# Two transformer layers in fp32: the last quarter of the tokens is transposed on VectorE instead of TensorE ahead of each feed-forward

## The chip, the core and the metric

The kernel runs on one core of a Trainium2 chip. A core has five engines with an instruction queue each: TensorE (PE in the profile; its weight loads are listed apart as PEld), VectorE (DVE), ScalarE (ACT), GpSimd (POOL) and SyncE (SP, which here only issues DMAs). Each engine works through its own queue in order and waits on semaphores for the others. The time is the device time of one execution in microseconds (us), the median of several runs.

## What is computed

Two layers, each attention with shared keys and values (16 query heads, one key/value head) and a SwiGLU feed-forward, both behind a layer norm and added to the residual. S = 2048 tokens, width D = 448, head width 28, feed-forward width F = 1792, all fp32.

```python
def _A_ref(x, wq, wk, wv, wo):                  # attention, one k and v for 16 heads
    q = (x @ wq).reshape(B, S, H, Dh).transpose(0, 2, 1, 3)
    k, v = x @ wk, x @ wv
    p = softmax(einsum("bhqd,bkd->bhqk", q, k) * Dh ** -0.5)
    return einsum("bhqk,bkd->bhqd", p, v).transpose(0, 2, 1, 3).reshape(B, S, H * Dh) @ wo

def _B_ref(x, w_gate, w_up, w_down):            # SwiGLU
    return (silu(x @ w_gate) * (x @ w_up)) @ w_down

x = A_x
for _ in range(2):                              # the same weights in both layers
    x = x + _A_ref(layernorm(x), wq, wk, wv, wo)
    x = x + _B_ref(layernorm(x), w_gate, w_up, w_down)
```

## The kernel before

**Numbers in two parts.** The products run on operands of a shortened fp32 type (fp32r in the rows), so each operand is split into a high part (`xh`, a cast) and a low part (`xl`, what the cast lost), and a product is three passes: high x high, high x low, low x high. To split a 512-token block is called halving it here (`halved`, lines L292 to L302: a cast and a subtraction for each of the quarters k = 0, 1, 2 of the width; for k = 3, only 64 rows wide, two casts and one subtraction).

**Tokens.** The residual `xres` stays in SBUF, tokens on the partitions, as 16 tiles of 128 x 448. Four tiles make a chunk c = 0 to 3 of 512 tokens. For the feed-forward a chunk has to be normed and transposed (width on the partitions). There are two ways. One goes over TensorE: `flip` transposes 128 x 128 blocks with an identity into a PSUM bank (L248), and ACT and VectorE halve from the bank (L254 to L264). The other goes over VectorE and DRAM: `turn_tile` transposes within 32 x 32 squares (L268), `send` writes the result to DRAM so that the squares land in place (L274, four DMAs), and `fetch` reads it back (`rows3`, L130 and L132). Tokens then stand in another order, and `natural` and `in_order` put them right with strided views where a bank is read.

**Norm.** `norm_steps` gives nine steps: statistics of four tiles (L217, L218 on VectorE), the scale on GpSimd (L222, L223), and the application to four tiles (L230, VectorE). Where the chunk goes over TensorE, GpSimd also copies 64 columns a second time behind each (L232).

**Feed-forward.** F is cut into 14 tiles fc of 128, two to a group gi (7 groups). The loops run over group, chunk and tile of the group: `unit(gi, c, n)` computes gate and up for one tile of F and one chunk into a pair of PSUM banks (L332, in two halves of 64 rows side by side; between them two one-element copies by ACT, L339, keep the order). Then ACT takes Silu (L1021), VectorE multiplies (L1022), ACT casts the high part (L1023), VectorE subtracts for the low part `h` (L1026). The down product of a unit (also L332, operands `wdh`, `wdl` and `h`) isn't issued at once: it is kept in `pend` and stands in the middle and at the end of the next unit. After the second tile of a group four banks hold a sum of 128 x 448 each, which is added to the residual: tiles 0 and 1 by VectorE (L892), tiles 2 and 3 by a copy of ACT (L895) and an addition of GpSimd (L896). These additions stand on their engines between the Silu work of the next unit.

**Banks.** PSUM has eight banks. Gate and up take turns over LOW = (0, 1, 2, 3), the down sums hold HIGH = (4, 5, 6, 7). `bank()` hands out the next bank of a list; TensorE waits there until its former user has let go.

**Order.** The schedule is written by hand: within an engine the instructions stand in the order of the code. `soon` holds steps that are run some units later, `mid` steps that stand in the middle of a certain unit, `plan` steps of the hand-over between the layers.

**Chunk 3.** Chunks 0 to 2 have gone over VectorE and DRAM during attention and are ready early. Chunk 3's residual is only complete when attention ends. In `rest`, at the start of the feed-forward, its statistics are taken; chunk 2 is halved by GpSimd (`parts(2)`); chunk 3 is applied two units later, by `soon`; and in the middle of unit (0, 2, 1), before and after the first half of the down product, TensorE transposes it (`turned`), two blocks of eight 128 x 128 blocks. The first unit that reads it is (0, 3, 0). Chunk 3 is therefore the only one whose tokens stand in the natural order (`sq` is false for it).

**Projections of layer 1.** During the last units of layer 0's feed-forward, and after it in `finish`, queries, keys and values of layer 1 are computed, 16 projections of 128 rows (`q`, products L312). Each holds one bank, which ACT copies out (and VectorE too, L546, where it holds a part of v). In `finish` of layer 1 the banks come from a list that begins with bank 0.

Of the kernel before, what the change touches and what calls it, by code (L numbers as in the profile page):

```python
# [55 lines left out]
def forward(  # L56
# [286 lines left out]
    class Attention:  # L343
# [79 lines left out]
        def parts(self, i):  # L423
            q = qts[i % 3]
            split(q[:, 0, :], q[:, 1, :], qraw)
# [86 lines left out]
        def turned(self, c):  # L512
            if c in self.norms:
                flip(self.norms.pop(c), self.X[c])

        def q(self, c, m):
            cs = slice(512 * c, 512 * c + 512)
            sq = c in self.squares
            held, po = bank((3, 4, 5) if self.seen > len(self.order) - 4 else wide[-1], True)
            ms = slice(P * m, P * m + P)  # L520
            wh, wl = self.w
# [31 lines left out]
        def finish(self):  # L553

            wide.append((0, 1, 2, 3, 4, 5, 6, 7) if self.layer else ALL)
            if self.layer:
# [280 lines left out]
    class FeedForward:  # L837
# [132 lines left out]

        def turned(self, c, ks=range(4)):
            if c not in self.X:
                self.X[c] = xtile(self.xbp, self.xd[c])
            flip(self.norms[c], self.X[c], ks)

        def flush(self):
# [5 lines left out]
        def unit(self, gi, c, n):  # L982
# [36 lines left out]
            sg = pers.tile([P, 512], F32, name="sg")  # L1019
            sq = c < NC - 1  # L1020
            nc.scalar.activation(in_order(sg, sq), natural(pg[0], sq), AF.Silu)  # L1021
            nc.vector.tensor_tensor(in_order(sg, sq), natural(pg[1], sq), in_order(sg, sq), ALU.mult)  # L1022
            nc.scalar.copy(hh, sg)  # L1023
# [34 lines left out]
        def rest(self, xb):  # L1058
# [4 lines left out]
            for c in range(2):  # L1063
                dma(self.xd[c][64:128, :], self.X[c][0][0:64, 3, :])
                self.X[c] = (*self.X[c][:2], self.xd[c])
            fs3, self.norms[3] = norm_steps(3)
            for f in fs3[:5]:
                f()
            self.parts(2, nc.gpsimd.tensor_copy, nc.gpsimd.tensor_tensor)
            self.soon.append([1, lambda: [f() for f in fs3[5:]]])  # L1070
            self.mid[0, 2, 1] = [lambda ks=ks: self.turned(3, ks) for ks in ((0, 1), (2, 3))]
            for gi, fs in enumerate(groups):
# [4 lines left out]
                for c in range(NC):  # L1077
                    for n in range(len(fs)):
                        if gi or c:
                            self.unit(gi, c, n)  # L1080
                if gi == len(groups) - 2 and self.nxt:
                    self.nxt.w = load_wqkv(xb.enter_context(tc.tile_pool(name="wqkv1", bufs=1, reuse_waits="tile")), None)[1]
# [87 lines left out]
```

## Times and profile before

| | us |
|---|---|
| median of 3 runs (lowest to highest) | 1957.98 (1957.88 to 1958.28) |
| profiled execution | 1958.55 |
| its span | 1956.8 |
| TensorE busy | 1942.8 (99%) |
| TensorE weight loads busy | 1328.7 (68%) |
| VectorE busy | 969.6 (50%) |
| ScalarE busy | 1262.7 (65%) |
| GpSimd busy | 553.9 (28%) |
| attention and projections of layer 0, 0 to 564: TensorE busy | 559.0 |
| feed-forward of layer 0, 564 to 974: TensorE busy | 409.2 of 410 |
| attention of layer 1, 974 to 1533: TensorE busy | 556.5 of 559 |
| feed-forward of layer 1 and end, 1533 to 1957: TensorE busy | 418.1 of 424 |

The limits of the four stretches are round numbers near the places where one kind of work ends and the next begins. The feed-forward of layer 1 repeats that of layer 0 about 968.8 us later, so one of them is read in detail and the other checked. Rows of the time order give start, duration, engine, line, operation, output and inputs; "x4" are four like instructions that follow each other, and "[0.36 <-DVE sg L1022]" is the time that the engine stood idle before the row and what released it. Ends of rows overlap the next start by some hundredths, since an engine starts the next instruction before the last one has drained.

### The profile page before, as it was taken

The numbers are of one execution on the slowest core, as the hardware profiler recorded it, in microseconds if no ns is written. First come the engines' busy times: TensorE is split into PE (matmuls) and PEld (weight loads), VectorE is DVE, ScalarE is ACT, GpSimd is POOL, SyncE is SP. The second block draws the span as 40 slices with busy tenths as digits, with TensorE's granted clock in tenths as the row PEclk, the third lists the DMA queues.
The fourth block names the chain that finished last, engine by engine and source line by source line (L and its number), as shares of the span: only waits on it lengthen the run. The fifth ranks groups of instructions, "written<-read, shape, count | busy, mean of one in ns | idle before, by whom it ended". The sixth has DMA issues, their size and how long they took to land. (4 is left out here: it accounts for less than half of the span.)

```text
span 1956.8 us, 43898 instructions
## 1 busy us (share of the span) xinstructions
PE 1942.8 (99%) x18425; PEld 1328.7 (68%) x18425; DVE 969.6 (50%) x1639; ACT 1262.7 (65%) x1877; POOL 553.9 (28%) x592
## 2 busy tenths in 40 slices
PE   9999999999999999999999999999999999999998
PEld 7544545445468999999974445454454789988887
DVE  6666575665643222322655555657656432232323
ACT  4899898998953333333349998989989333333332
POOL 4213123122214333433341221122231342333420
PEclk9999999999999999999999999999999999999999
DMA  5111011121130011100251110110221201011102
GB/s 167 55 35 30 21 39 41 27 55 39 25 87 25 17 32 32 33 22 22 70 156 36 34 34 20 42 38 24 57 50 32 72 18 31 17 32 32 32 1 77
DMA packets 100642, 83.60 MB, mean 43 GB/s; under 512 B 25080, under 2 KB 81656, under 8 KB 100440
## 3 DMA queue, kind: packets, MB, share of 16 engines
q1 hardware_dynamic: 98744, 79.32, 14.7%
q8 instruction: 145, 2.38, 0.5%
q10 hardware_dynamic: 1696, 1.43, 0.2%
q14 instruction: 57, 0.47, 0.1%
HBM read 57.38 MB, written 21.50 MB: 40 GB/s over the span
## 5 line engine op out<-in xcount | busy, mean ns | idle before, releaser
L655 ACT ACTIVATE pt<-three 128x1536 f32<-128x1536 f32 x512 | 726.9, 1499 | 52.8 <-PE three L633 52.8
L688 PE MATMUL bank<-pt,vsb 128*32 128x512 f32 x3072 | 490.8, 598 | 0.0
L688 PE MATMUL bank<-pair,vsb 128*32 128x512 f32 x1024 | 487.4, 598 | 0.6 <-ACT pair L656 0.6
L633 PE MATMUL bank<-qstack,keys 32*128 32x512 f32 x1536 | 473.3, 425 | 0.0
L332 PE MATMUL bank<-xh,wgh 64*128 64x512 f32 x1712 | 446.7, 389 | 0.0
L633 PE MATMUL three<-qstack,keys 32*128 32x512 f32 x4608 | 428.6, 408 | 0.5 <-ACT xn L539 0.3
L633 PEld LDWEIGHTS bank<-qstack,keys 32*128 32x128 f32 x1536 | 243.3, 183 | 250.4 <-issue 123.3
L654 DVE COPY pair<-bank 128x512 f32<-128x512 f32 x512 | 354.2, 692 | 95.2 <-PE bank L633 58.9
L332 PE MATMUL bank<-xh,wgl 64*128 64x512 f32 x1391 | 368.3, 390 | 0.0
L332 PE MATMUL bank<-xl,wgh 64*128 64x512 f32 x1284 | 335.2, 389 | 0.0
L332 PE MATMUL bank<-wdh,h 64*128 64x448 f32 x1760 | 328.3, 363 | 0.0
L1022 DVE TENSOR_TENSOR sg<-bank,sg 128x512 f32<-128x512 f32 x112 | 77.4, 691 | 500.7 <-ACT sg L1021 495.8
L656 ACT ACTIVATE pair<-pair 128x1024 f32<-128x1024 f32 x256 | 285.4, 1115 | 0.0
L332 PEld LDWEIGHTS bank<-xh,wgh 64*128 64x128 f32 x1712 | 265.1, 184 | 15.6 <-issue 1.3
L633 PEld LDWEIGHTS three<-qstack,keys 32*128 32x128 f32 x4608 | 261.0, 183 | 13.9 <-DVE xres L604 1.5
L688 PEld LDWEIGHTS bank<-pt,vsb 128*32 128x32 f32 x3072 | 101.7, 109 | 246.2 <-issue 153.2
L896 POOL TENSOR_TENSOR xres<-stage,xres 128x448 f32<-128x448 f32 x107 | 126.5, 1204 | 492.8 <-ACT stage L895 492.6
L697 DVE TENSOR_TENSOR o<-bank,o 128x512 f32<-128x512 f32 x224 | 154.9, 692 | 203.7 <-PE bank L688 203.7
L332 PEld LDWEIGHTS bank<-wdh,h 64*128 64x128 f32 x1760 | 244.6, 184 | 11.6 <-issue 2.0
L339 ACT COPY seen<-bank 128x1 f32<-128x1 f32 x654 | 80.7, 163 | 250.4 <-PE bank L332 247.5
L332 PEld LDWEIGHTS bank<-xh,wgl 64*128 64x128 f32 x1391 | 218.1, 184 | 13.4
L332 PE MATMUL bank<-wdl,h 64*128 64x448 f32 x880 | 218.3, 366 | 0.0
(149 smaller groups left out, 2118.8 us busy)
## 6 DMA issues: line engine op xcount, KB each, us to landing
o<-rd SPq DMA_DIRECT2D x32, 256.0 KB
qraw<-qd SPq DMA_DIRECT2D x128, 56.0 KB
qd<-stage SPq DMA_DIRECT2D x28, 224.0 KB
wdr<-in_B_w_down_dram SPq DMA_DIRECT2D x28, 224.0 KB
xt<-tb SPq DMA_DIRECT2D x24, 224.0 KB
wr<-in_B_w_gate_dram SPq DMA_DIRECT2D x28, 192.0 KB
wr<-in_B_w_up_dram SPq DMA_DIRECT2D x28, 192.0 KB
xn<-xt SPq DMA_DIRECT2D x6, 768.0 KB
```

Source lines behind the costliest of these rows:

```text
L332: nc.tensor.matmul(po, a, b, start=start, stop=stop, skip_group_check=True)
L339: nc.scalar.copy(seen[:, i : i + 1], po[:, 0:1])
L633: nc.tensor.matmul(three[:, j, :] if j < 3 else one, k[js, kp, ks], q[js, part, :], start=(z == 0), stop=(z == 2), tile_position=(32 * j, 0),)
L654: copies.append(nc.vector.tensor_copy(pt1, one))
L655: es.append(nc.scalar.activation(pt, threes[y], AF.Exp, scale=SCALE))
L656: es.append(nc.scalar.activation(pair, pair, AF.Exp, scale=SCALE))
L688: nc.tensor.matmul(to[32 * j : 32 * j + 32, :], vsb[:, n % NT, :], pts[n][j], start=(y == 0), stop=(y == 1), skip_group_check=True,)
L697: f = nc.vector.tensor_tensor(accs[i][:, 0, :], to, accs[i][:, 0, :], ALU.add)
L896: nc.gpsimd.tensor_tensor(r, s, r, ALU.add)
L1022: nc.vector.tensor_tensor(in_order(sg, sq), natural(pg[1], sq), in_order(sg, sq), ALU.mult)
```

## The change

Chunk 3 takes the other way, over VectorE and DRAM, in both layers. In `rest` a pool of its own (`t3`) is opened for the transposed tile `tb3`, for the normed tile `xn`, and for a one-element tile `applied`. VectorE applies the norm right behind the statistics and the scale, and transposes the four tiles at once. Four DMAs send them to DRAM. GpSimd copies one element of the last normed tile to `applied`, ahead of `parts(2)`, so that its halving of chunk 2 waits until VectorE has applied all four tiles. One unit later `fetch(3)` is issued on SP's queue; it reads into the tile from which chunk 2 is halved. Two units after that GpSimd halves the quarters k = 2, 3 of chunk 3; in the middle of unit (0, 2, 1) ACT and VectorE halve k = 0, 1. The transposes on TensorE, with the method `turned`, are gone; Silu and product read all chunks by the strided views. The pool is closed after group 0.

The second part: `q` keeps the number of the bank that it used last, and in `finish` of layer 1 the list of the LOW banks begins with the one after it.

```diff
@@ class Attention: q
             held, po = bank((3, 4, 5) if self.seen > len(self.order) - 4 else wide[-1], True)
+            self.used = held
@@ finish
-            wide.append((0, 1, 2, 3, 4, 5, 6, 7) if self.layer else ALL)
+            wide.append((*((self.used + n) % 4 for n in range(1, 5)), *HIGH) if self.layer else ALL)
@@ class FeedForward
-        def turned(self, c, ks=range(4)):
-            if c not in self.X:
-                self.X[c] = xtile(self.xbp, self.xd[c])
-            flip(self.norms[c], self.X[c], ks)
@@ unit
-            sq = c < NC - 1
-            nc.scalar.activation(in_order(sg, sq), natural(pg[0], sq), AF.Silu)
-            nc.vector.tensor_tensor(in_order(sg, sq), natural(pg[1], sq), in_order(sg, sq), ALU.mult)
+            nc.scalar.activation(in_order(sg, True), natural(pg[0], True), AF.Silu)
+            nc.vector.tensor_tensor(in_order(sg, True), natural(pg[1], True), in_order(sg, True), ALU.mult)
@@ rest
-            fs3, self.norms[3] = norm_steps(3)
+            t3 = ExitStack()
+            own = t3.enter_context(tc.tile_pool(name=f"t3{self.layer}", bufs=1, reuse_waits="tile"))
+            tb = own.tile([P, D // 32, P], F32, name="tb3")
+            fs3, got = norm_steps(3, own, twice=False)
             for f in fs3[:5]:
                 f()
+            for f in fs3[5:]:
+                f()
+            for t in range(4):
+                turn_tile(got, tb, t)
+            self.raw[3] = dram.tile([D, 512], F32, name=f"xt{self.layer}_3")
+            send(tb, self.raw[3])
+            nc.gpsimd.tensor_copy(own.tile([P, 1], F32, name="applied"), got["x"][:, 3, 0:1])
             self.parts(2, nc.gpsimd.tensor_copy, nc.gpsimd.tensor_tensor)
-            self.soon.append([1, lambda: [f() for f in fs3[5:]]])
-            self.mid[0, 2, 1] = [lambda ks=ks: self.turned(3, ks) for ks in ((0, 1), (2, 3))]
+
+            def parts(ks, copy, sub):
+                if 3 not in self.X:
+                    self.X[3] = xtile(self.xbp, self.xd[3])
+                halved(self.X[3], self.got[3], ks, copy, sub)
+
+            self.soon.append([0, lambda: self.fetch(3)])
+            self.soon.append([2, lambda: parts((2, 3), nc.gpsimd.tensor_copy, nc.gpsimd.tensor_tensor)])
+            self.mid[0, 2, 1] = [lambda: parts((0, 1), nc.scalar.copy, nc.vector.tensor_tensor)]
...
+                if gi == 0:
+                    t3.close()
```

How the instructions then stand can be seen on two engines. (In the changed file the same statements of `unit` and `accumulate` have other line numbers: the product L1022 is L1017 there, L1026 is L1021, L892 is L893, L896 is L897. `bank_6435` to `bank_6438` are LOW, `h_...` the low parts of the units in turn, `sg` the gate, `mv` the statistics.) VectorE before, from the last statistics of chunk 3 in layer 0 over units (0, 1, 0), (0, 1, 1) and the beginning of (0, 2, 0):

```order
L218 BN_AGGR mv<-stats 128x2
L1022 TENSOR_TENSOR sg<-bank_6437,sg 128x512
L892 TENSOR_TENSOR xres<-bank_6439,xres 128x448
L1026 TENSOR_TENSOR h_6708<-sg,h_6708 128x512
L892 TENSOR_TENSOR xres<-bank_6440,xres 128x448
L1022 TENSOR_TENSOR sg<-bank_6435,sg 128x512
L1026 TENSOR_TENSOR h_6794<-sg,h_6794 128x512
L230 TENSOR_SCALAR xn<-xres,mv,rstd 128x448 x4
```

VectorE after, from the same place:

```order
L218 BN_AGGR mv<-stats 128x2
L230 TENSOR_SCALAR xn<-xres,mv,rstd 128x448 x4
L268 STREAM_TRANSPOSE tb_6629<-xn 128x14x32 x4
L1017 TENSOR_TENSOR sg<-bank_6437,sg 128x512
L893 TENSOR_TENSOR xres<-bank_6439,xres 128x448
L1021 TENSOR_TENSOR h_6728<-sg,h_6728 128x512
```

The application has moved ahead of the product of unit (0, 1, 0), of the additions behind chunk 0's first group, and of that unit's low part; four transposes, which VectorE did not have here before, stand behind it.

GpSimd before, from the scale of chunk 3 (L223) to the first weights of the next group (L135); `xn` is what the halving reads, `stage` the copies of the down sums:

```order
L223 TENSOR_TENSOR rstd<-rstd,halfn 128x4
L292 CAST xh<-xn 128x512
L293 TENSOR_TENSOR xl<-xn,xh 128x512
...
L299 CAST xd_6622<-xn 64x512
L300 CAST xh<-xn 64x512
L302 TENSOR_TENSOR xh<-xn,xd_6622 64x512
L896 TENSOR_TENSOR xres<-stage,xres 128x448 x2
L232 COPY xn<-xn 128x64 x4
L896 TENSOR_TENSOR xres<-stage,xres 128x448 x4
L135 TENSOR_SCALAR wgh<-wr 128x1024
```

GpSimd after, from the same place (the left-out rows are those of the other quarters of chunk 2, the same as before):

```order
L223 TENSOR_TENSOR rstd<-rstd,halfn 128x4
L1073 COPY applied<-xn 128x1
...
L302 TENSOR_TENSOR xh<-xn,xd_6622 64x512
L897 TENSOR_TENSOR xres<-stage,xres 128x448 x4
L292 CAST xh<-xn 128x512
L293 TENSOR_TENSOR xl<-xn,xh 128x512
L299 CAST xd_6623<-xn 64x512
L300 CAST xh<-xn 64x512
L302 TENSOR_TENSOR xh<-xn,xd_6623 64x512
L897 TENSOR_TENSOR xres<-stage,xres 128x448 x2
L135 TENSOR_SCALAR wgh<-wr 128x1024
```

The copy to `applied` stands ahead of chunk 2's halving, the second copy of 64 columns is gone, and the halves k = 2, 3 of chunk 3 stand behind the additions of chunk 1 and ahead of those of chunk 2.

On SP's queue the four sends and the three DMAs of `fetch(3)` stand behind the two DMAs that move 64 rows of chunks 0 and 1 (L127), and ahead of the weights of the next tiles of F:

```order
L127 DMA xd_6621<-xh 64x512
L274 DMA xt_3_6650<-tb_6629 32x14x128 x4
L130 DMA xn<-xt_3_6650 128x3x512
L132 DMA xn<-xt_3_6650 64x512 x2
L130 DMA wr<-in_B_w_gate_dram 128x3x128
```

Before, the last row followed the first directly.

## Prediction

> **What bounds the kernel now.** I read the page's totals first, then a table by stretches, cut where VectorE starts each unit's gate product (L1022), then the order of time on each engine around chunk 3. (Columns of the table: stretch in us, its length, and each engine's busy time in it.)
>
> ```profile
> span 1956.8 us, 43898 instructions
> PE 1942.8 (99%) x18425; PEld 1328.7 (68%) x18425; DVE 969.6 (50%) x1639; ACT 1262.7 (65%) x1877; POOL 553.9 (28%) x592
> ...
> core 0: us, PE busy (x) PEld busy (x) DVE busy (x) ACT busy (x) POOL busy (x), PEclk, DMA share, GB/s
> ...
> 596.98:604.28 7.30, 7.30 (x70) 6.64 (x68) 3.08 (x7) 1.99 (x8) 2.77 (x6) 1.00 0.01 2
> 604.28:614.01 9.73, 9.73 (x85) 7.84 (x83) 5.12 (x8) 5.56 (x15) 2.35 (x2) 1.00 0.00 0
> 614.01:621.79 7.78, 7.78 (x71) 6.78 (x69) 1.38 (x2) 1.98 (x8) 0.00 (x0) 1.00 0.01 3
> 621.79:629.08 7.29, 7.29 (x70) 6.79 (x68) 2.45 (x4) 2.86 (x10) 5.35 (x4) 1.00 0.01 2
> ...
> 1573.08:1582.82 9.74, 9.74 (x85) 7.75 (x83) 5.13 (x9) 5.57 (x15) 2.34 (x2) 1.00 0.00 1
> 1582.82:1590.58 7.76, 7.76 (x71) 6.65 (x69) 1.39 (x3) 1.99 (x8) 0.00 (x0) 1.00 0.01 2
> ```
>
> TensorE is busy in 99% of the span, at full clock (1.00): the time is its instruction stream plus its waits, and another engine's work counts only where TensorE waits for it. A feed-forward unit takes 7.29 us. The one in which chunk 3 is transposed, (0,2,1), takes 9.73, and the next, (0,3,0), 7.78: 9.73 + 7.78 - 2 x 7.29 = 2.93 us too much in layer 0, 2.92 in layer 1. The weight loads show why:
>
> ```profile
> 607.28 0.85 PEld L248 LDWEIGHTS bank<-ident,xn 128*128 128x128 f32 x8 [0.35 <-issue]
> ...
> 609.74 0.86 PEld L248 LDWEIGHTS bank<-ident,xn 128*128 128x128 f32 x8 [0.31 <-issue]
> ...
> 614.76 0.18 PEld L332 LDWEIGHTS bank<-xh,wgh 64*128 64x128 f32 x1 [0.36 <-DVE sg L1022]
> ```
>
> There are two blocks of eight transposes, with a gap at each end; and unit (0,3,0) waits for VectorE's L1022, because the transposes shifted the turn of the banks, so that it got the pair which the unit before it still held.
>
> **1. TensorE loses 16 transposes per layer.** Nothing replaces them on TensorE. Both causes go, the blocks and the bank conflict: in the new order the pairs alternate again. Gain 2.93 + 2.92 = 5.85 us.
>
> **2. VectorE applies and turns chunk 3 at once.** Now its order is statistics, four L230, four L268, and only then unit (0,1,0)'s L1022. Before:
>
> ```profile
> 585.47 0.18 DVE L218 BATCH_NORM_AGGREGATE mv<-stats 128x2 f32<-128x6 f32 x1
> 589.69 0.69 DVE L1022 TENSOR_TENSOR sg<-bank,sg 128x512 f32<-128x512 f32 x1 [4.04 <-ACT sg L1021]
> ...
> 591.07 0.94 DVE L1026 TENSOR_TENSOR h<-sg,h 128x512 fp32r<-128x512 f32 x1 [0.15 <-ACT h L1023]
> 591.92 0.61 DVE L892 TENSOR_TENSOR xres<-bank,xres 128x448 f32<-128x448 f32 x1
> ...
> 951.98 1.77 DVE L230 TENSOR_SCALAR xn<-xres,mv,rstd 128x448 f32<-128x448 f32 x4
> 953.67 2.22 DVE L268 STREAM_TRANSPOSE xh<-xn 128x448 f32<-128x448 f32 x4
> ...
> 586.02 1.02 POOL L223 TENSOR_TENSOR rstd<-rstd,halfn 128x4 f32<-128x4 f32 x1
> 586.99 0.61 POOL L292 CAST xh<-xn 128x512 fp32r<-128x512 f32 x1
> ...
> 589.60 1.30 POOL L293 TENSOR_TENSOR xl<-xn,xh 128x512 fp32r<-128x512 f32 x1
> 590.84 0.62 POOL L292 CAST xh<-xn 128x512 fp32r<-128x512 f32 x1
> ...
> 594.58 1.29 POOL L302 TENSOR_TENSOR xh<-xn,xd 64x512 fp32r<-64x512 f32 x1
> ...
> L232 POOL COPY xn<-xn x28: 238/454/459, 9.4 to 1569.6; 128x64 f32<-128x64 f32 x28
> ```
>
> L223 ends at 587.04, so L230 can start at about 587.07. The same eight instructions took 953.67 + 2.22 - 951.98 = 3.91 us in the hand-over between layers, so they end at 590.98. L1022 starts at about 590.95 (a follower starts some hundredths before the end shown) instead of 589.69: 1.26 late. L1026 then asks to start at 591.07 + 1.26 = 592.33.
>
> GpSimd waits too: its one-element copy runs after the last L230 (587.07 + 1.77 = 588.84). No row has that shape. The nearest is the 64-wide copy of L232, 0.24 to 0.46 us; I take 0.20, a little under its fastest, with ends 0.05 and 0.46. Chunk 2's split then starts near 589.1 instead of 586.99, 2.1 late, and its second L293, from 589.60 before, now runs from 591.7 to 593.0: L1026 meets it. What a meeting costs the rows show:
>
> ```profile
> 630.46 1.63 DVE L1026 TENSOR_TENSOR h<-sg,h 128x512 fp32r<-128x512 f32 x1 [0.69 <-ACT h L1023]
> ...
> 630.38 1.16 POOL L136 TENSOR_TENSOR wdl<-wdr,wdh 128x448 fp32r<-128x448 f32 x1
> ...
> 592.39 0.38 PEld L332 LDWEIGHTS bank<-wdh,h 64*128 64x128 f32 x2
> ...
> 592.79 0.22 PEld L332 LDWEIGHTS bank<-wdh,h 64*128 64x128 f32 x2
> ...
> 632.14 0.47 PEld L332 LDWEIGHTS bank<-wdh,h 64*128 64x128 f32 x4
> ```
>
> L1026 takes 0.69 when it meets nothing (two L1026 and L1022 make the 1.38 of the row 614.01). At 630.46 it ended at 632.09, 0.55 after the GpSimd instruction that it met (630.38 + 1.16 = 631.54). So here it ends at 593.0 + 0.55 = 593.55, and the L892 behind it at 594.08 instead of 592.53 (it starts 0.08 before the other's end and takes 0.61). TensorE's down product reads L1026's result in the second load of the row 592.39, at 592.59, and writes L892's bank from 592.79. With 0.05 for the signal (632.14 - 632.09) this load comes at 594.13, 1.34 late. Some lateness is free, because loads run ahead of the products: the load at 632.14 came 0.16 late by the units' pitch of 7.29, and its unit was no longer for it. Price: 1.34 - 0.16 = **1.18 us per layer**. Ends: 0.62 if L1026 meets nothing; 1.56 if it takes the whole 1.63 and L892 follows.
>
> The Trainium skill, page "SBUF — State Buffer", section "Who interferes with whom", says that a VectorE instruction with two SBUF inputs and a GpSimd one that reads SBUF shut each other out for the whole instruction, and that a VectorE instruction with one SBUF input is left alone outside the fast modes. By this rule the meeting at 630.46 is as it should be, and the turning itself (L268, one input) would not be held by the split beside it; the sum by the rule is the one above.
>
> **3. GpSimd and ACT split chunk 3 from memory.** Its way: L274 sends it, L130 and L132 fetch it, ACT and VectorE split two quarters, GpSimd the others, behind chunk 1's L896.
>
> ```profile
> 994.00 3.02 SPq L274 DMA_DIRECT2D xt<-xh  x4
> ...
> 1001.58 0.39 SPq L945 DMA_DIRECT2D qstack<-xt  x1
> ...
> 552.38 0.44 SPq L130 DMA_DIRECT2D xn<-xt  x1
> ...
> 557.33 1.66 ACT L292 CAST xh<-xn 128x512 fp32r<-128x512 f32 x3 [0.48 <-DMA xn<-xt]
> ...
> 606.13 2.35 POOL L896 TENSOR_TENSOR xres<-stage,xres 128x448 f32<-128x448 f32 x2 [5.08 <-ACT stage L895]
> 625.96 1.07 POOL L135 TENSOR_SCALAR wgh<-wr 128x1024 fp32r<-128x1024 f32 x1
> ...
> 607.23 0.38 ACT L339 COPY seen<-bank 128x1 f32<-128x1 f32 x2 [0.74 <-PE bank L332]
> ...
> 583.25 0.60 SPq L130 DMA_DIRECT2D wr<-in_B_w_gate_dram  x1
> ...
> 599.23 0.18 PEld L332 LDWEIGHTS bank<-xh,wgh 64*128 64x128 f32 x1
> ```
>
> From a send to the fetch behind it took 1001.58 - 994.00 = 7.6 us, so the fetch can issue at 590.98 + 7.6 = 598.6; its buffer is chunk 2's, which GpSimd gives up at 595.87 + 2.2 = 598.1. It lands 4.95 later (552.38 to 557.33), at 603.6. ACT asks at about 608.9 (where its copies of the unit's middle stood, 607.23 + 0.38, plus the 1.2) and GpSimd at 609.65 (chunk 1's last L896, 608.48, plus 1.2): 5 us to spare. GpSimd's five instructions took 5.03, from 590.84 to 595.87, with one meeting of 0.33 in it (a L293 of 1.62 instead of 1.29); from 609.65, with two meetings of 0.4 with VectorE's own halves, they end near 609.65 + 4.7 + 0.8 = 615.15. TensorE needs the last of them where 599.23 stood, two units and the 1.2 on: 615.01, of which again 0.16 is free. That is level; I take 0.1 us per layer, ends 0 and 0.9 (two more meetings).
>
> On SP's queue the weights of F-tile 3 stand behind the fetch, so they leave at about 600 instead of 583.25; GpSimd splits them only at 625.96, so nothing waits. ACT's two casts replace five. Chunk 3's Silu and product read their banks by strides now as those of chunks 0 to 2 did, which took the same 0.69: nothing. The send (L274) costs SP's queue 3.0 us of issue and nobody else.
>
> **4. Banks of layer 1.** Before, chunk 3's second projection in the hand-over gets bank 3, which chunk 2's last projection holds until its L546:
>
> ```profile
> 1023.45 0.19 PEld L312 LDWEIGHTS bank<-xh,wl 128*128 128x128 f32 x1
> 1024.17 0.19 PEld L312 LDWEIGHTS bank<-xh,wh 128*128 128x128 f32 x1 [0.53 <-DVE vt L546]
> ```
>
> At the pitch of these loads, 0.23, it was due at 1023.68, and came 0.49 late. Now chunk 2's last projection has bank 0 and the wait goes: 0.49 less the free 0.16, gain 0.3 (ends 0 and 0.5). The other turns keep their distance.
>
> **Sum.** -5.85 - 0.3 + 2 x 1.18 + 2 x 0.1 = -3.6 us. The profiled execution took 1958.55 (span 1956.8), which gives 1954.95; it lies 0.57 above the median of 1957.98, so the median becomes **1954.4** (0.18% less). With every end good, 5.85 + 0.5 - 2 x 0.62 = 5.1 is gained: 1952.9. With every end bad, 5.85 - 2 x 1.56 - 2 x 0.9 = 0.9: 1957.1.
>
> **Rivals.** (a) VectorE's lateness costs nothing, since the loads have more room than I see: 1957.98 - 6.15 = 1951.8. Against it stand the loads at 592.59 and 592.79, only 0.6 and 0.3 behind the ends of L1026 (592.01) and L892 (592.53). Chance 0.08. (b) L1026 misses GpSimd's split, if that stands 0.65 later or 0.67 earlier than I put it: 2 x 0.56 more is gained, 1953.3. The copy's price would have to be 0.85, twice that of the 64-wide one, or the start of L230 that much off. Chance 0.12. (c) GpSimd is late with chunk 3 by the bad end of part 3, 0.9 instead of 0.1: 1956.0. Chance 0.10. (d) The end on the other side: the way through memory is late. Each us by which the fetch lands after 609.65 is a us of TensorE in unit (0,3,0), per layer; from 611.45 on the 3.6 is eaten up, and at 614, 10.4 later than reckoned, it gives 1954.4 + 2 x 4.35 = 1963.1. For it speaks that the fetch waits for four sends and that the weights' queue has one blocked head; against it the 7.6 and 4.95 above. Chance 0.10. (e) My forecast: 0.60, its own range 1952.9 to 1957.1.
>
> **Numbers.** Within 0.2% (3.9 us, about what a measurement of this kernel tells from no change) means 1954.1 to 1961.9. The forecast's spread straddles the lower edge: 0.22 of its 0.60 below, 0.38 within. Faster 0.22 + 0.08 + 0.12 = 0.42; same 0.38 + 0.10 = 0.48; slower 0.10. The range 1952.4 to 1957.8 leaves out (a) and (d), 0.18.
>
> **What would show it.** No L248 in the feed-forward; every unit from (0,2,0) on at 7.29; one stretch of about 8.5 where 589.69 stood, with a weight load of L332 waiting for VectorE's L892 or L1026; L268 ending near 591; an L1026 of 1.2 us or so; chunk 3's last GpSimd L302 near 615. A wait of unit (0,3,0) on GpSimd, ACT or a DMA, or a stretch well under 8 in that place, proves a step wrong.

## The result, and the profile after

| | before | after |
|---|---|---|
| median, us (22 runs each) | 1958.49 | 1954.68 |
| lowest to highest | 1957.73 to 1963.68 | 1952.88 to 1957.93 |
| ratio after / before, 95% interval | | 0.9979 (0.9973 to 0.9985) |
| profiled execution | 1958.55 | 1957.93 |
| its span | 1956.8 | 1956.2 |

The change is faster: by 3.8 us between the medians, by 0.21% in the ratio. A gain of 3.6 us was predicted, to 1954.4 from the 1957.98 of the first three runs. Two of the twelve executions of the change's second series, reported below, ran at a granted TensorE clock of 0.85 and 0.56 and took 2108 and 3068 us; no median and no ratio in what follows counts them. The profiled execution after is the slowest of its 22, 3.25 above their median, so its whole span says little. It has to be read by stretches. First VectorE (DVE) and GpSimd (POOL) of the changed kernel in layer 0, around units (0,1,0) and (0,1,1); columns are start, duration, engine, line, operation. (L1017 is the product that was L1022, L1021 the low part that was L1026, L893 the addition that was L892.)

```profile
586.51 0.18 DVE L218 BATCH_NORM_AGGREGATE mv<-stats 128x2 f32<-128x6 f32 x1
588.12 1.78 DVE L230 TENSOR_SCALAR xn<-xres,mv,rstd 128x448 f32<-128x448 f32 x4 [1.42 <-POOL rstd L223]
589.82 2.21 DVE L268 STREAM_TRANSPOSE tb<-xn 128x448 f32<-128x448 f32 x4
591.96 0.65 DVE L1017 TENSOR_TENSOR sg<-bank,sg 128x512 f32<-128x512 f32 x1
...
593.29 1.34 DVE L1021 TENSOR_TENSOR h<-sg,h 128x512 fp32r<-128x512 f32 x1 [0.16 <-ACT h L1018]
594.56 0.61 DVE L893 TENSOR_TENSOR xres<-bank,xres 128x448 f32<-128x448 f32 x1
599.10 0.69 DVE L1017 TENSOR_TENSOR sg<-bank,sg 128x512 f32<-128x512 f32 x1 [3.93 <-ACT sg L1016]
...
590.03 0.19 POOL L1073 COPY applied<-xn 128x1 f32<-128x1 f32 x1 [1.95 <-DVE xn L230]
...
592.79 1.30 POOL L293 TENSOR_TENSOR xl<-xn,xh 128x512 fp32r<-128x512 f32 x1
...
614.75 1.29 POOL L302 TENSOR_TENSOR xh<-xn,xd 64x512 fp32r<-64x512 f32 x1
```

Everything here is 1.04 later than in the profile before (586.51 against 585.47), since this execution started later; all comparisons below take that off. L230 and L268 run without a gap, and L1017 starts 1.23 late (591.96 - 589.69 - 1.04). L1021 meets GpSimd's L293 and takes 1.34. TensorE's weight loads (PEld) wait for both, where before nothing waited:

```profile
594.69 0.19 PEld L332 LDWEIGHTS bank<-wdh,h 64*128 64x128 f32 x2 [0.65 <-DVE h L1021]
595.22 0.19 PEld L332 LDWEIGHTS bank<-wdh,h 64*128 64x128 f32 x2 [0.35 <-DVE xres L893]
```

From the last statistics to unit (0,1,1)'s product it is 599.10 - 586.51 = 12.59 us, against 596.98 - 585.47 = 11.51 before: 1.08 us of stall. Then the units by stretches (stretch, its length, and each engine's busy time in it), from product to product:

```profile
591.96:599.10 7.14, 6.81 (x59) 5.32 (x57) 3.05 (x6) 2.65 (x10) 6.78 (x8) 1.00 0.54 129
599.10:606.39 7.29, 7.29 (x70) 7.09 (x68) 2.30 (x2) 1.91 (x8) 2.36 (x3) 1.00 0.87 233
606.39:613.68 7.29, 7.29 (x70) 7.09 (x67) 4.29 (x6) 3.62 (x12) 5.29 (x5) 1.00 0.06 18
613.68:621.02 7.34, 7.34 (x70) 7.26 (x68) 2.21 (x3) 2.00 (x8) 2.22 (x3) 1.00 0.01 3
```

Where chunk 3 was transposed stand 7.29 and 7.34 in place of 9.73 and 7.78. The 0.05 in the 7.34 is probably chunk 3's last halving, which ends at 616.04 (614.75 + 1.29), 615.00 on the old clock; no weight load there waits long enough to be listed, and one later profile (three tiles turned later, again; layer 1) has a unit of 7.37 with a load that waited 0.22 us for this L302. The way through memory is no matter: the sends leave from 592.06, the fetch at 599.20, and ACT's two casts at 609.67 stand behind its copies for TensorE and wait for no DMA.

```profile
592.06 3.01 SPq L274 DMA_DIRECT2D xt<-tb  x4
599.20 0.38 SPq L130 DMA_DIRECT2D xn<-xt  x1
...
609.67 1.15 ACT L292 CAST xh<-xn 128x512 fp32r<-128x512 f32 x2
```

The same sum can be taken over a whole feed-forward, from the last statistics of chunk 3 to the last gate product. In layer 1 these two rows are, before and after:

```profile
1554.28 0.18 DVE L218 BATCH_NORM_AGGREGATE mv<-stats 128x2 f32<-128x6 f32 x1
...
1946.97 0.69 DVE L1022 TENSOR_TENSOR sg<-bank,sg 128x512 f32<-128x512 f32 x1 [2.77 <-PE bank L312]
```

```profile
1555.48 0.18 DVE L218 BATCH_NORM_AGGREGATE mv<-stats 128x2 f32<-128x6 f32 x1
...
1946.35 0.69 DVE L1017 TENSOR_TENSOR sg<-bank,sg 128x512 f32<-128x512 f32 x1 [2.76 <-PE bank L312]
```

392.69 and 390.87: 1.82 us less. Layer 0 has 399.14 and 397.34, 1.80 less. Twice that is 3.6, the gain of the medians.

Why then was this execution so slow? It lost 1.2 us ahead of the first scores (65.14 against 63.92) and 2.0 us at the hand-over (50.30 against 48.26), where TensorE waits for chunk 2's fetch (cast by ACT's L292, subtracted by VectorE's L293). Before and after, weight loads and then stretches of 2 us with the granted clock (the last but two figure):

```profile
1006.13 0.19 PEld L312 LDWEIGHTS bank<-xh,wh 128*128 128x128 f32 x1 [1.71 <-ACT xh L292]
1007.24 0.29 PEld L312 LDWEIGHTS bank<-xl,wh 128*128 128x128 f32 x1 [0.92 <-DVE xl L293]
...
1008.00:1010.00 2.00, 2.00 (x7) 1.52 (x6) 1.17 (x2) 0.85 (x2) 1.26 (x2) 0.50 0.54 180
1010.00:1012.00 2.00, 2.00 (x9) 1.65 (x8) 0.00 (x0) 0.29 (x1) 0.69 (x2) 0.86 0.47 151
```

```profile
1007.14 0.28 PEld L312 LDWEIGHTS bank<-xh,wh 128*128 128x128 f32 x1 [3.48 <-ACT xh L292]
1007.87 0.29 PEld L312 LDWEIGHTS bank<-xl,wh 128*128 128x128 f32 x1 [0.44 <-DVE xl L293]
...
1008.00:1010.00 2.00, 2.00 (x5) 1.61 (x6) 1.74 (x3) 1.43 (x3) 0.00 (x0) 0.50 0.68 224
1010.00:1012.00 2.00, 2.00 (x6) 1.52 (x6) 0.00 (x0) 0.07 (x1) 0.56 (x1) 0.50 0.43 134
1012.00:1014.00 2.00, 2.00 (x7) 1.57 (x6) 0.72 (x1) 1.59 (x3) 1.78 (x4) 0.62 0.35 108
```

The wait was longer (3.48 against 1.71), and behind it TensorE ran at half its clock for 6.8 us instead of 3.4. Whether the change does that was the first thing to find out.

### The profile page after: what moved, and what is told of

Same layout as the page of the kernel before. It is cut to its first block, busy times and chain, and to the rows that moved or that the text cites. A ratio compares the mean times of both kernels' runs of the same rounds, so it can differ in the third digit from the quotient of the medians.

```text
span 1956.2 us, 43857 instructions
## 1 busy us (share of the span) xinstructions
PE 1938.9 (99%) x18393; PEld 1335.2 (68%) x18393; DVE 976.9 (50%) x1643; ACT 1252.7 (64%) x1871; POOL 559.6 (29%) x596
## 5 line engine op out<-in xcount | busy, mean ns | idle before, releaser
L332 PE MATMUL bank<-xh,wgh 64*128 64x512 f32 x1712 | 375.8, 389 | 0.0
L332 PE MATMUL bank<-xh,wgl 64*128 64x512 f32 x1391 | 324.1, 390 | 0.0
L1017 DVE TENSOR_TENSOR sg<-bank,sg 128x512 f32<-128x512 f32 x112 | 77.4, 691 | 491.0 <-ACT sg L1016 486.1
L332 PE MATMUL bank<-wdh,h 64*128 64x448 f32 x1760 | 311.6, 363 | 0.8 <-DVE h L1021 0.5
L332 PE MATMUL bank<-xl,wgh 64*128 64x512 f32 x1284 | 282.3, 389 | 0.0
L897 POOL TENSOR_TENSOR xres<-stage,xres 128x448 f32<-128x448 f32 x107 | 126.4, 1202 | 480.0 <-ACT stage L896 479.7
L339 ACT COPY seen<-bank 128x1 f32<-128x1 f32 x654 | 74.9, 164 | 259.3 <-PE bank L332 258.5
L332 PEld LDWEIGHTS bank<-xh,wgh 64*128 64x128 f32 x1712 | 200.5, 184 | 12.2 <-issue 1.0
L332 PEld LDWEIGHTS bank<-wdh,h 64*128 64x128 f32 x1760 | 198.1, 184 | 11.6 <-issue 1.7
L1016 ACT ACTIVATE sg<-bank 128x512 f32<-128x512 f32 x112 | 67.3, 601 | 214.7 <-PE bank L332 211.5
L332 PE MATMUL bank<-wdl,h 64*128 64x448 f32 x880 | 184.1, 367 | 0.0
```

What stands on the lines that cost most here:

```text
L332: nc.tensor.matmul(po, a, b, start=start, stop=stop, skip_group_check=True)
L339: nc.scalar.copy(seen[:, i : i + 1], po[:, 0:1])
L897: nc.gpsimd.tensor_tensor(r, s, r, ALU.add)
L1016: nc.scalar.activation(in_order(sg, True), natural(pg[0], True), AF.Silu)
L1017: nc.vector.tensor_tensor(in_order(sg, True), natural(pg[1], True), in_order(sg, True), ALU.mult)
```

## The experiments

All times are read against runs of the kernel before on the same chip, since its median differed from chip to chip (it was 1958.55, 1959.3 and 1959.86 in the three groups below). The table gives four stretches of each profiled execution, worked out from the time order: to the first scores of layer 0; feed-forward 0 and 1 as above; and the hand-over, from the end of feed-forward 0 to the first scores of layer 1. The last column is the ratio with its interval. The two attentions and the end, left out, differ by under 0.9 us each.

| kernel | first scores | feed-forward 0 | hand-over | feed-forward 1 | ratio to before |
|---|---|---|---|---|---|
| before | 63.92 | 399.15 | 48.26 | 392.70 | |
| before, again | 63.93 | 399.12 | 48.95 | 392.71 | 0.9998 (0.9989 to 1.0007) |
| after | 65.14 | 397.34 | 50.30 | 390.87 | 0.9979 (0.9973 to 0.9985) |
| after, again | 64.44 | 397.97 | 47.30 | 390.86 | 0.9981 (0.9972 to 0.9990) |
| after, third | 65.72 | 397.29 | 48.72 | 390.86 | 0.9981 (0.9972 to 0.9990) |
| three tiles turned later | 64.02 | 396.65 | 46.85 | 389.85 | 0.9975 (0.9965 to 0.9984) |
| the same, again | 64.17 | 396.30 | 48.73 | 389.89 | 0.9966 (0.9954 to 0.9978) |
| GpSimd does not wait | 64.28 | 403.41 | 47.91 | 394.90 | 1.0033 (1.0023 to 1.0043) |
| old list of banks | 64.11 | 397.33 | 48.64 | 390.86 | 0.9984 (0.9975 to 0.9992) |
| chunk 2 zero | 65.64 | 396.91 | 48.69 | 390.26 | one run |
| 2 transposes twice | 64.35 | 398.10 | 48.65 | 391.45 | 0.9984 (0.9974 to 0.9993) |
| 4 transposes twice | 65.29 | 401.12 | 48.68 | 392.85 | 1.0006 (0.9997 to 1.0016) |
| later, and early load | 64.28 | 396.84 | 49.07 | 389.85 | 0.9965 (0.9951 to 0.9978) |

### The kernels once more

The kernel after was run a second time, and later a third time beside the one before, unchanged.

> The changed kernel once more, for a second profile, because the first profiled execution (1957.93) lies 3.25 above the median of 1954.68. Theory A (the waits for the hand-over's chunk 2 differ from execution to execution; in the first profile TensorE stood 3.06 us at 1004.09, released by ACT's L292, which waited for the load of qstack, against 1.29 and 0.61 before): the two stretches around chunk 3 repeat to within 0.1 us (stall of the unit that stood at 589.69 about 1.1 per layer, each feed-forward 1.8 shorter than before), and the gap at the hand-over is another length, near 1.5 to 2 in an execution of 1954.5. Rival B (the change itself makes the load late by 2 us, always): the gap is 3 us again and the profiled time is near 1957.9. Time against before: 0.9980 by either.

> The kernel before once more, for a second profile. Read by stretches (from the last statistics of chunk 3 to the last gate product of each feed-forward; from there to the first scores of layer 1, the hand-over). Theory A (the change shortens each feed-forward by 1.8 us and leaves the hand-over as it was, which differs by itself from execution to execution: 46.9 to 50.3 us in ten profiles of these kernels): the feed-forward of layer 1 takes 392.7 again, the hand-over anything from 46.8 to 50.3. Rival B (the change also alters the hand-over): the hand-over is under 47, outside what the changed kernels show, and the gain is less than the feed-forwards' sum.

> The change a third time, beside the next kernel and the one before on the same chip. Theory A: feed-forward of layer 1 390.86 again, hand-over and start as they fall, time 0.9980 of before. Rival B (the first two profiles differ by the place of the wait): another feed-forward by over 0.2 us.

Theory A held, but for one figure. Feed-forward 1 repeats to 0.01 us for either kernel. Feed-forward 0 of the second profile of the change is only 1.2 shorter than before, not 1.8: the rest went in its last two units, where projections of layer 1 already run and which took 20.74 us there, 20.05 and 20.04 in the other two profiles. Up to those units, from the last statistics to the third-last gate product, feed-forward 0 takes 379.11 and 379.09 before and 377.29, 377.22 and 377.26 after.

The hand-over does not repeat: 47.3 to 50.3 after, 48.3 and 48.9 before. In all five profiles the fetch of chunk 2 leaves SP's queue 16.95 to 16.97 us behind the end of feed-forward 0; ACT's casts, which wait for it, start 3.89 us after that in both profiles before and 5.66, 4.01 and 5.28 us after it in those of the change. So the long wait is not the first profile's alone, and the start too is longer in every profile of a changed kernel (64.02 to 65.72) than in the two before. Two profiles are too few to say that the change has no part in this. The medians say that the part is small: the three profiled executions of the change lie 3.25, 0.2 and 1.5 above their medians, those before within 0.2 of theirs, and the change's medians lie 3.8, 3.7 and 3.4 us under those before, about what the feed-forwards alone give (3.6 to 3.7). The second profile of the change:

```profile
1005.34 0.19 PEld L312 LDWEIGHTS bank<-xh,wh 128*128 128x128 f32 x1 [1.84 <-ACT xh L292]
1006.29 0.19 PEld L312 LDWEIGHTS bank<-xl,wh 128*128 128x128 f32 x1 [0.77 <-DVE xl L293]
...
1008.00:1010.00 2.00, 2.00 (x9) 1.42 (x8) 0.25 (x1) 0.00 (x0) 0.35 (x1) 1.00 0.30 105
```

Here the wait is that of before, and the clock stays at 1.00. It stays there in the second profile before too, behind waits of 1.73 and 0.90 us, where in the first it fell behind 1.71 and 0.92:

```profile
1008.00:1010.00 2.00, 2.00 (x10) 1.46 (x9) 1.23 (x2) 0.66 (x2) 1.28 (x2) 1.00 0.61 199
```

### What the stall is made of: three tiles turned later

```diff
-            for t in range(4):
-                turn_tile(got, tb, t)
+            turn_tile(got, tb, 0)
             self.raw[3] = dram.tile([D, 512], F32, name=f"xt{self.layer}_3")
-            send(tb, self.raw[3])
+            def turn_rest():
+                for t in range(1, 4):
+                    turn_tile(got, tb, t)
+                send(tb, self.raw[3])
+            self.soon.append([0, turn_rest])
```

> The change with one tile of chunk 3 turned ahead of unit (0,1,0)'s product and the other three behind that unit's last addition. Theory A (the stall of about 1.1 us per layer comes from the block of 3.9 us on VectorE ahead of that product): the product starts on time, L1021 asks 1.2 earlier and meets the first L293 of GpSimd's halving (0.55 behind its end at the most), the loads of the down product wait 0 to 0.2, and the time falls by 1.8 to 2.2 us against the change: about 1952.6, ratio to before 0.9969. The send is some 3.3 us later, the fetch lands near 607.5 in place of 604, still ahead of ACT at about 608. Rival B (the stall is GpSimd's halving alone, which holds L1021 wherever it stands): the stall stays at 0.5 to 1, time 1954. Rival C (the later fetch is late for ACT or GpSimd): a wait of unit (0,3,0), 0.5 to 2 us per layer, time 1954 to 1957.

> The kernel with three of the tiles turned later once more, beside the change itself on the same chip. Theory A (the stall of about 1.0 us per layer is all that the earlier block cost): feed-forward of layer 1 389.85, 1.0 less than the change; median 2.0 us under that of the change, ratio to before 0.9970. Rival B (the gain seen in the first run was that of a short hand-over): median within 0.7 us of the change.

```profile
588.60 0.64 DVE L268 STREAM_TRANSPOSE tb<-xn 128x448 f32<-128x448 f32 x1
589.52 0.69 DVE L1017 TENSOR_TENSOR sg<-bank,sg 128x512 f32<-128x512 f32 x1 [0.29 <-ACT sg L1016]
...
590.90 1.14 DVE L1021 TENSOR_TENSOR h<-sg,h 128x512 fp32r<-128x512 f32 x1 [0.16 <-ACT h L1018]
...
592.50 1.68 DVE L268 STREAM_TRANSPOSE tb<-xn 128x448 f32<-128x448 f32 x3
596.82 0.69 DVE L1017 TENSOR_TENSOR sg<-bank,sg 128x512 f32<-128x512 f32 x1 [2.64 <-ACT sg L1016]
```

The product waits for ACT again instead of for the transposes, and the next one follows 7.30 later. L1021 still meets GpSimd (1.14) and it costs nothing. Feed-forward 1 is 1.0 shorter than after the change and 2.85 shorter than before: nearly the whole 2.92 of its two long units. Feed-forward 0, up to the third-last product, takes 376.22 and 376.21, again 1.0 less than after the change. Theory A in the trace; the medians, 1953.50 and 1953.67, are 1.4 and 2.8 us under those of the change on the same chips (1954.9 and 1956.46). This version beats the kernel before clearly, and the change by the trace; of the runs, the second series stands apart (its slowest is 1954.40, the fastest of the change there 1955.09), the first does not.

### What the stall is made of: GpSimd's part

In one kernel GpSimd writes zeros in place of halving chunk 2.

```diff
-            self.parts(2, nc.gpsimd.tensor_copy, nc.gpsimd.tensor_tensor)
+            self.X[2] = xtile(self.xbp, self.xd[2])
+            self.got.pop(2)
+            for z in (...):                       # all parts of chunk 2
+                nc.gpsimd.memset(z.bitcast(F32), 0.0)
```

> The change without the halving of chunk 2: GpSimd writes zeros instead, so chunk 2's feed-forward is left out of the result, and no GpSimd instruction reads SBUF beside VectorE at unit (0,1,0). Theory A (the 1.02 us by which that unit is late in the second profile of the change are made of VectorE's block, 1.23 late, and of L1021's meeting with GpSimd's L293, 0.6): L1021 takes 0.69 in place of 1.31, the loads come 0.5 earlier, and the unit is late by 0.4 to 0.6. Rival B (the meeting costs nothing more, since L1021 would wait as long for ACT or VectorE's queue): L1021 is as long, or the unit is late by 1.0 all the same. Rival C (zeros hold VectorE as well, writing alone is enough): L1021 above 1.

```profile
592.30 0.65 DVE L1017 TENSOR_TENSOR sg<-bank,sg 128x512 f32<-128x512 f32 x1
...
593.65 0.69 DVE L1021 TENSOR_TENSOR h<-sg,h 128x512 fp32r<-128x512 f32 x1 [0.16 <-ACT h L1018]
...
593.77 0.53 POOL L1077 MEMSET xd<- 128x512 f32 x1
```

Beside GpSimd instructions that only write, L1021 takes 0.69. Feed-forward 1 is 0.60 shorter than after the change. So of the 1.02 of stall (12.53 - 11.51 in the second profile of the change) some 0.4 belongs to VectorE's block and 0.6 to the meeting. (The prediction's rule for the meeting, taken from 630.46, holds: around chunk 3, in all thirteen profiles, each of the 37 of these subtractions that took longer than 0.72 us ended 0.54 to 0.55 us behind the GpSimd instruction that it met.) The Trainium skill, page "SBUF — State Buffer", section "Who interferes with whom", says that an instruction with two SBUF inputs contends with a GpSimd one that reads, not with one that only writes; these rows agree.

In the other kernel the one-element copy is left out, so that GpSimd halves chunk 2 beside the application.

```diff
-            nc.gpsimd.tensor_copy(own.tile([P, 1], F32, name="applied"), got["x"][:, 3, 0:1])
```

> The change without the one-element copy, so GpSimd halves chunk 2 right behind the scale, beside VectorE's application and turning. Theory A (an application is held for the rest of a GpSimd instruction that it meets, as L232 and L230 hold each other up: L232 takes 0.24 at its fastest and 0.46 beside L230): the four L230 take 3 to 4.5 us in place of 1.78, the product of unit (0,1,0) starts 1 to 2.5 us later, and the stall of about 1.1 grows to 2 to 3.5 per layer: 1956.5 to 1959.5. Rival B (they do not hold each other): VectorE's block stays at 3.91, GpSimd ends its halving 2.0 us earlier, the L1021 of that unit meets the third L293 in place of the second, and the time is that of the change, within 0.5 us: 1954.2 to 1955.2.

```profile
587.29 4.29 DVE L230 TENSOR_SCALAR xn<-xres,mv,rstd 128x448 f32<-128x448 f32 x4 [1.43 <-POOL rstd L223]
591.51 2.21 DVE L268 STREAM_TRANSPOSE tb<-xn 128x448 f32<-128x448 f32 x4
...
587.90 1.31 POOL L293 TENSOR_TENSOR xl<-xn,xh 128x512 fp32r<-128x512 f32 x1
...
595.00 0.18 PEld L332 LDWEIGHTS bank<-wdh,h 64*128 64x128 f32 x1 [2.45 <-ACT h L1018]
...
596.72 0.29 PEld L332 LDWEIGHTS bank<-wdh,h 64*128 64x128 f32 x2 [0.99 <-DVE h L1021]
...
598.00:600.00 2.00, 2.00 (x12) 1.64 (x12) 0.00 (x0) 0.29 (x3) 0.79 (x1) 0.50 0.52 135
600.00:602.00 2.00, 2.00 (x14) 1.53 (x12) 0.00 (x0) 0.00 (x0) 0.00 (x0) 0.50 0.40 49
```

Theory A's mechanism: the four L230 take 4.29 instead of 1.78, while the transposes beside the same GpSimd instructions keep their 2.21. The cost was beyond both theories: 1964.91 against 1954.9, 10.0 us (the expectations below say 9.6). The feed-forwards give 5.5 (up to the third-last product of layer 0, 382.79 against 377.26) and 4.0 of it (394.90 against 390.86). The block is 2.5 longer and L1021 takes 1.68; most of the rest is TensorE's clock, at 0.50 for 6.8 us in layer 0 (596.2 to 603.0) behind gaps of 2.03 and 0.61 us, and for 3.4 us in layer 1 behind gaps of 1.95 and 0.62. The two layers differ by 1.5 us, and in the clock by those 3.4 us more at half speed. So the small wait on GpSimd, of which the prediction counted only the price, decides the sign: without it the changed kernel is 0.33% slower than the kernel before. The same section of the Trainium skill says that an operation such as L230's can run in a mode that takes the shared ports and then blocks GpSimd or is blocked by it; the L230 rows agree, and the 2.21 of L268 is what the prediction said of an instruction with one SBUF input.

### A longer block, and the clock

Two, then four of the transposes were done twice, to lengthen VectorE's block alone.

```diff
+            for t in range(2):                    # 4 in the other kernel
+                turn_tile(got, tb, t)
             for t in range(4):
                 turn_tile(got, tb, t)
```

> The change with two of the four transposes done twice, so VectorE's block ahead of unit (0,1,0)'s product is 2 x 0.53 = 1.06 us longer. Theory A (the stall grows one to one with the block): the gap of 0.25 in TensorE's stream becomes 1.3, the time rises by 2 x 1.06 = 2.1 us, to 1957, ratio to before 0.9992. Rival B (a gap that long halves TensorE's granted clock for some us, as after the gaps of 2.03 and 0.61 us where GpSimd did not wait: 0.50 from 598 to 602 there): granted clock 0.50 behind the gap, the time rises by 2 x (1.06 + 3) = 8 us, to 1963.

> The change with all four transposes done twice, a block longer by 4 x 0.53 = 2.13 us. Theory A (one to one): the time rises by 4.3 us against the change, to 1959.2, ratio to before 1.0004. Rival B (a gap above 2 us halves the granted clock for 6 us, as in the kernel in which GpSimd did not wait, where a block 2.5 longer cost 9.6 us in all): granted clock 0.50 for about 6 us behind the gap, 3 us more per layer, 1965, ratio 1.0033.

With two, the ratio is 0.9984 against the change's 0.9981, and feed-forward 1 grows by 0.59: less than Theory A's 1.06, since L1021, 1.08 later, now meets the shorter cast behind the subtraction (0.85 against 1.31):

```profile
593.58 0.85 DVE L1021 TENSOR_TENSOR h<-sg,h 128x512 fp32r<-128x512 f32 x1 [0.15 <-ACT h L1018]
```

TensorE's gap there is 0.56 us, and no clock below 1.00 follows it. With four the ratio rises by 0.0025, 4.9 us, near Theory A's 4.3; but the trace shows the two layers apart. Feed-forward 1 grows by 1.99, feed-forward 0 by 3.5 up to its third-last product (380.77 against 377.26):

```profile
595.52 0.18 PEld L332 LDWEIGHTS bank<-wdh,h 64*128 64x128 f32 x1 [2.04 <-ACT h L1018]
...
598.00:600.00 2.00, 2.00 (x12) 1.59 (x12) 0.00 (x0) 0.29 (x3) 1.92 (x2) 0.50 0.78 206
...
1568.00:1570.00 2.00, 1.87 (x15) 1.23 (x14) 0.80 (x2) 0.42 (x6) 1.86 (x3) 1.00 0.87 196
1570.00:1572.00 2.00, 2.00 (x20) 1.60 (x20) 0.00 (x0) 0.12 (x2) 1.92 (x3) 1.00 0.59 153
```

The gaps in TensorE's products are alike (1.62 us in layer 0, 1.59 in layer 1), and the clock fell to half behind one, for 3.4 us (597.7 to 601.1), and not behind the other. Theory A holds in layer 1; layer 0 shows Rival B's halved clock, for 3.4 us instead of 6, and pays 1.5 us for it. The Trainium skill, page "TensorE: Matmul & The Clock Gate", speaks in its Part 1 of a free-running window of about 3.4 us over which activity is judged. The traces agree on its length: where GpSimd did not wait, the clock changes at 596.20, 603.02, 1012.62, 1016.04, 1569.00 and 1572.41, which are 2, 120, 1, 162 and 1 steps of 3.413 us apart, and in the other traces too every change stands whole steps from the others. That the same gap falls differently goes with a window that runs freely; that 1.6 us are enough does not go with an idle time of 3.4, and here the measurement decides. How much idle time in a step is enough stays open: with four transposes twice, TensorE's products fill 0.61 of the step ahead of the fall in layer 0, and in 0.55 of a step in layer 1 behind which the clock did not fall.

### The banks

```diff
-            wide.append((*((self.used + n) % 4 for n in range(1, 5)), *HIGH) if self.layer else ALL)
+            wide.append((0, 1, 2, 3, 4, 5, 6, 7) if self.layer else ALL)
```

> The change with the old list of banks in the finish of layer 1. Theory A (the second part of the change removes one wait of a projection for VectorE's L547, 0.1 to 0.5 us): the wait of 0.53 is back at chunk 3's second projection, near 1024, with a gap of TensorE of 0.1 there, and the time is 0.1 to 0.5 above that of the change, too little to be told apart. Rival B (the old list collides with the banks that the feed-forward's end leaves in another turn): a new gap of 0.5 to 1.5 us at the first projection of the finish, near 993.

```profile
992.86 0.19 PEld L312 LDWEIGHTS bank<-xh,wh 128*128 128x128 f32 x1 [1.49 <-DVE vt L547]
...
1022.65 0.19 PEld L312 LDWEIGHTS bank<-xh,wh 128*128 128x128 f32 x1 [1.32 <-DVE vt L547]
```

Both theories' waits are there, the one near 1024 and a new one at the first projection of the finish: gaps of 0.89 and 1.11 us in the products. Neither is in the three profiles of the change. Yet the time can't be told apart (0.9984 against 0.9981; medians 1955.71 and 1954.9) and the hand-over, 48.64, inside the spread of the others: the loads of chunk 2 wait for its transfer, which lands when it lands, and the gap before them was 0.60 here against 1.42 in the change's second profile, so part of the 1.11 was taken out of that wait. What the edit is worth stays open, between nothing and 2 us.

### An earlier load for the hand-over

To the kernel with three tiles turned later, the hand-over's chunk 2 was turned and sent right behind its statistics, and fetched a unit later instead of in the finish.

```diff
+            if c == 2:
+                for f in fs[5:]:
+                    f()
+                tb = self.xbp.tile([P, 4, 512], F32R, name="xh").bitcast(F32)
...
+                for t in range(4):
+                    turn_tile(got, tb, t)
+                send(tb, to)
+                def take():
+                    a.X[2] = xtile(self.xbp)
+                    load()
+                self.soon.append([1, take])
+                a.plan[7, 0] = [parts]
+                return
             self.soon.append([1, turn])
-            if c == 2:
-                a.plan[4, 1] = [load]
-                a.plan[7, 0] = [parts]
-                return
```

> The kernel with three tiles turned later, and besides the hand-over's chunk 2 is applied, turned and sent right behind its statistics (VectorE is idle there from 978.5 to 983.9 in the first profile of the change) and fetched one unit later, ahead of the projections' stores on SP's queue, instead of behind them near 1001. Theory A (TensorE's two gaps at the hand-over, 1.25 and 0.64 us with three tiles turned later, 3.06 in the slow profile of the change, are the wait for this fetch): both are gone, the load of qstack is there some 8 us ahead, the time falls by 1.9 us or more against the kernel with three tiles turned later: 1951 to 1951.7, ratio to before 0.9964, and the single executions spread less than the 4 us there. Rival B (the projections of chunk 2 then wait for something else: the stores of SP's queue, which stand 3 us later behind the sends, or chunk 0's maxima): the gap stays above 1 us or stands elsewhere, time 1953 to 1954.

The casts of chunk 2 ran at 1002.14 without waiting for the fetch, but its subtraction stood on VectorE behind other work of the hand-over, and TensorE stood 1.88 us for it in place of the fetch; and the sends on SP's queue held up the projections' stores, for which ACT waited 3.27 us, and behind it TensorE 1.65, near 990. The wait for the subtraction, in the weight loads:

```profile
1006.23 0.19 PEld L312 LDWEIGHTS bank<-xl,wh 128*128 128x128 f32 x1 [2.31 <-DVE xl L293]
```

By the waits this is Rival B: one was removed and two came. The hand-over took 49.07. The time does not decide: the ratio, 0.9965, is near Theory A's 0.9964, but does not stand apart from 0.9975 and 0.9966 without this edit.

## Why the prediction was right

**Step 1, 5.85 us.** Right. The units stand at 7.29 and 7.34 where 9.73 and 7.78 stood, and where the new stall is taken away too, feed-forward 1 is 2.85 shorter, of 2.92, and feed-forward 0, up to the third-last product, 2.89, of 2.93. How much belongs to the blocks and how much to the turn of the banks no run tells apart.

**Step 2, 1.18 us per layer.** Right to 0.2: 1.08 and 1.02. The sign given for it, a stretch of about 8.5 where 589.69 stood, has to be counted from there: L1017 itself is 1.23 late, so that it is only 7.14 from product to product, but 8.37 from the old place of the first (599.10 - 1.04 - 589.69). The parts fit as well. The block ends 3.91 after the start of L230; L1017 was predicted 1.26 late and is 1.23; the second L893 was to end at 594.08, which is 595.12 on this clock, and ends at 595.17; the copy took 0.19 (0.20 taken). (The two ends, 0.62 and 1.56, come out as 0.65 and 1.59 when worked like the middle; nothing hangs on it.) The split into block and meeting was 0.62 + 0.56 and measured 0.4 + 0.6, so the free lateness was taken some 0.2 too small, and the meeting too cheap by less than 0.1. A price that depends on such a meeting is no constant: with a block 1.06 longer L1021 met 0.46 less.

**Step 3.** Right: chunk 3's last L302 ended at 615.00 on the old clock (615.15 predicted), and the unit was 0.05 longer (0.1), if that is its cause. The fetch left at 598.16 on that clock (598.6).

**Step 4, banks, a gain of 0.3.** Not shown. It was sized from one profile, and the wait is not the same in each: a weight load waited there 0.53 us in the first profile before and 1.89 in the second. The change has no such wait, but its worth drowns in the hand-over.

```profile
1024.98 0.19 PEld L312 LDWEIGHTS bank<-xh,wh 128*128 128x128 f32 x1 [1.89 <-DVE vt L546]
```

**The sum.** -3.6 predicted; 1.82 and 1.80 from the two feed-forwards, 3.6 in all, and 3.8 from the medians. That the figures meet so closely is in part luck: of the 3.6 predicted, 0.3 stood for the banks, which no run shows, and only 3.3 for the feed-forwards. They gave some 0.35 more, since step 2 was 0.1 to 0.16 too dear per layer and step 3 by 0.05, and this made up for the banks. The profiled time of 1957.93 would have looked like a miss: the prediction took the start and the hand-over as equal in all executions, and said nothing of them. They differ by 1.8 and 3.5 us in the profiles here, as much as the gain, and only stretches that leave them out show it.

**The rivals.** (a), no cost of VectorE's lateness: refuted by the waits at 594.69 and 595.22 and the 1.08 us behind them. (b), L1021 misses the split: it took 1.34 and met it. (c) and (d), GpSimd or the fetch late: 0.05 us and nothing.

## What to carry to other kernels

Before moving work onto an engine that is half idle, find the first instruction behind the new block for which the bound engine waits, and cut the block there: here one transpose ahead of it and three behind cost less than 0.1 us per layer, four ahead 1.0 us. Where two engines' instructions can hold each other, an ordering wait may be worth far more than it costs: here a copy of 0.19 us, for which GpSimd stood 1.95 us, was worth 10 us, some 5 of them the longer block itself (2.5 per layer) and most of the rest the halved clock of TensorE behind it. Compare stretches between two fixed instructions before comparing spans: stretches in which TensorE waits for no transfer repeated to 0.07 us or better in 377 (layer 0, up to the third-last product) and 0.01 in 391 (layer 1), where whole executions spread over 5.

## What was not expected of the hardware

- The granted clock of TensorE can fall to half behind gaps of 1.3 to 3.1 us, for 3.4 or 6.8 us, and need not: a gap of 1.62 us was followed by 0.50 and one of 1.59 in the same execution by 1.00; in the hand-over it fell behind waits of the weight loads of 1.71 and 0.92 us (the first profile before) and not behind 1.73 and 0.90 (the second of the same kernel). Its changes stand whole steps of 3.41 us apart in each trace; which gap brings one was not settled.
- Four applications of the norm beside GpSimd's casts and subtractions took 4.29 us instead of 1.78, four transposes beside the same 2.21, as alone.
- A subtraction on VectorE with both inputs in SBUF, 0.69 us alone, ended 0.54 to 0.55 us behind the GpSimd instruction that it met, wherever the two began (37 cases), and took 0.69 beside GpSimd memsets.
